# Turning the last keys right behind the result: two small TensorE jobs of one unit put into one run

## The chip, the cores and the metric

One core of a Trainium2 chip runs the whole program. The metric is the device time of one execution in microseconds (us), as the median of several executions. Beside it there is one profiled execution, in which the start and length of every instruction are recorded.

## The reference

Two stages follow each other. The first is a gated linear attention: for each of 4 batches and 8 heads a 48x48 state runs over 768 tokens. The second is a mixture of four two-layer networks on the first stage's result, 3072 rows of 384.

```python
for t in range(S):                                    # B, H, S, D = 4, 8, 768, 48
    state = alpha[:, :, t, :, None] * state + einsum('bhd,bhe->bhde', k[:, :, t], v[:, :, t])
    y[:, :, t] = einsum('bhd,bhde->bhe', q[:, :, t], state)
...
p = domain_probs / (domain_probs.sum(-1, keepdims=True) + 1e-09)
for e in range(4):                                    # x: (3072, 384), w1: 384x1024, w2: 1024x384
    h = np.maximum(x @ w1[e], 0.0)
    out += p[:, e:e + 1] * (h @ w2[e])
```

## The kernel before

**Two kinds of work on one TensorE.** The tokens are cut into 24 units (6 blocks of 128 tokens times 4 batches), numbered from 0 here, so the eleventh unit is unit 10. Units form groups of 2, 4, 4, 4, 4, 4 and 2. The network works through one group after another, for each of the four experts an up layer (`up`, products L775 of 512 columns into `one`) and a down layer (`down`, products L847 of 384 columns into `ops`). The attention of the later units is spread between these products. Where the network is at work, TensorE executes long stretches of L775 and L847, and every few microseconds a short run of attention products.

**The attention of one unit** is a generator with 17 steps, `attention(u)`. Each `yield` ends a step. The steps that matter here, by their number:

- steps 3 to 6 and 8 to 10 prepare levels of decayed queries and keys. ScalarE copies queries into `qb` (L541) and keys into `KT` (L559), VectorE multiplies (L548, L550, L560).
- step 7 makes the products of four levels (L567, 64 matrix passes in the trace, called P below), and step 11 those of the far half (L623, F) and of two levels more (L567).
- steps 12 and 13 copy `far` and `near` into `lat` on ScalarE (L636, L640).
- step 14, `turn_keys`: four turns of the last keys on TensorE (L287, T) into a PSUM tile, and a copy of it into `AT` on ScalarE (L683). It does nothing for the last block of a batch (units 20 to 23).
- step 15, `result`: the products of the unit's result (L662, R), which read `lat`, the queries and the state, and a copy of the result on ScalarE into `x_raw` (L675), or into `AT` in the last group (L679).
- step 16: the product of the turned keys and the values (L697, S), four VectorE operations that bring the state up to date (L707, L708), and the load of the values for two units later on SyncE's DMA queue.

T, R, S, F and P name these runs below. A number behind a letter is the count of matrix passes that the trace shows: T4, R56, S8 (or S16, where two halves are made apart), F8 and P64 or P32.

**When a step is issued** is worked out in advance. `deal()` gives every step of every unit a due time as a share of the unit's span: step 13 at 0.80, 14 at 0.87, 15 at 0.94 and 16 at 1.0 (`BEATS`), or 0.67, 0.755, 0.84 and 1.02 for units 11 to 17 (`IN_PAIRS`). `TOGETHER = ((15, 7), (16, 11))` sets, for these units, the due time of the next unit's step 7 to that of this unit's step 15, and of the next unit's step 11 to that of this unit's step 16. The steps are sorted by due time, and `advance` issues them as the estimated cost of the network's products passes. Nothing else reorders: every engine executes its instructions in the order in which they were issued.

**Buffers on the way.** The PSUM tiles of T, R and S share two buffers (tag `w`). `x_raw` has one buffer: the first copy of a group's result waits until `split_x` (L734 on ScalarE, L271 on VectorE) has read the group before. `attention` sets `in_runs = 10`, from which unit on the inputs are loaded as runs and transposed by VectorE (L488).

Of the kernel before, what the change touches and what calls it, by code (L numbers as in the profile page):

```python
# [20 lines left out]
def kernel(  # L21
# [94 lines left out]
    half = B // 2  # L116
# [47 lines left out]
    in_runs = 10  # L164
# [119 lines left out]
    def turned(src):  # L284
        tp = ps.tile([P, NP, P], F32, name="tp", tag="w")
        for p in range(NP):
            nc.tensor.transpose(tp[:, p, :], src(p), ident)  # L287
        return tp
# [187 lines left out]
    def attention(u):  # L476
# [171 lines left out]
        def result():  # L648
            yps = ps.tile([P, KC, P], F32, name="yps", tag="w")
            strips = [[] for _ in range(P // QUAD)]  # L650
            for c in range(KC):
                for j, strip in enumerate(strips):
                    p, part = divmod(len(strips) * c + j, 3)
                    terms = [(flat_st[:, p, QUAD * part:QUAD * (part + 1)], QT[:, p, :])] if cb > 0 else []
                    for i in range(2):
                        if part != 2 * (1 - i):
                            at = VD * (2 * p + i) + QUAD * part - D * i
                            terms.append((flat_v[:, at:at + QUAD], lat[:, 2 * p + i, :]))
                    strip += [(c, n == 0, n == len(terms) - 1, *term) for n, term in enumerate(terms)]
            for turn in zip(*strips):  # L660
                for j, (c, begins, ends, lhsT, rhs) in enumerate(turn):
                    nc.tensor.matmul(yps[QUAD * j:QUAD * (j + 1), c, :], lhsT=lhsT, rhs=rhs,  # L662
                                     start=begins, stop=ends)
            gi, slot = place[cb, b]
            if slot == 0:
                if gi == 0:
                    xTs[gi] = work.tile([P, 3, KC, NT], F32R, name="xT", bufs=1)
                    xraws[gi] = xTs[gi][:, 2].bitcast(F32)
                elif gi < LAST:
                    xraws[gi] = work.tile([P, KC * NT + PAD], F32, name="x_raw", bufs=1)[:, :KC * NT]  # L670
                    xraws[gi] = xraws[gi].rearrange("p (c n) -> p c n", n=NT)
                else:
                    xraws[gi] = []
            if gi < LAST:
                nc.scalar.copy(out=xraws[gi][:, :, slot * P:(slot + 1) * P], in_=yps)  # L675
            else:

                xraws[gi].append(AT)
                nc.scalar.copy(out=AT[:, :KC, :], in_=yps)  # L679

        def turn_keys():
            if cb < NCB - 1:
                nc.scalar.copy(out=AT, in_=turned(lambda p: KT[:, p, :]))  # L683


        for step in (turn_keys, result) if u >= half else (result, turn_keys):
            step()
            yield

        if cb < NCB - 1:  # L690
            KB = AT
# [203 lines left out]
    def deal():  # L895
# [15 lines left out]
        for gis in [*([gi] for gi in range(1, LAST - 1)), [LAST - 1, LAST]]:  # L911
# [6 lines left out]
            for k in range(n):  # L918
                u = sum(map(len, groups[:gi])) + k
                end = due - (n - 1 - k) * space  # L920
                begin = max(end - 2 * space, ends[-2])
                ends.append(end)
                run = attention(u)
                pairs = u in in_pairs
                beats = [0.0, *(IN_PAIRS if pairs else BEATS)]
                due_at = {-1: begin, **{j: begin + (end - begin) * beats[j + 1] for j in (7, 11, 16)}}
                for ahead, j in TOGETHER if pairs else ():
                    if (u > in_pairs[0] or j == 11) and abs(times[-1][ahead] - due_at[j]) < space / 6:
                        due_at[j] = times[-1][ahead]

                marks = sorted(due_at)
                times.append([])
                for lo, hi in zip(marks, marks[1:]):
                    times[-1] += [due_at[hi] if j == hi else
                                  due_at[lo] + (due_at[hi] - due_at[lo]) * (beats[j + 1] - beats[lo + 1])
                                  / (beats[hi + 1] - beats[lo + 1]) for j in range(lo + 1, hi + 1)]

                for j, ahead in ((6, 13), (12, 15)):
                    if times[:-1]:
                        times[-1][j] = max(times[-1][j], times[-2][ahead] + 0.5)  # L940
                events += [(time, u, run) for time in times[-1]]
# [8 lines left out]
    with tc.manual_schedule():  # L950
# [22 lines left out]
        def fill(times, n=P):  # L973
            for _ in range(times):
                nc.tensor.matmul(idle[:, :n], lhsT=zeros[:, :P], rhs=zeros[:, :n], start=True, stop=True)

        runs = [None, attention(1)]
        fill(7)
        runs[0] = first_unit(fill, runs[1])
# [65 lines left out]
```

## Time and profile before

| | |
|---|---|
| median of 3 executions | 1033.85 us (1030.1 to 1035.3) |
| profiled execution | 1027.61 us, of which the span is 1025.7 us |
| granted TensorE clock, mean | 0.998 |
| busy share: TensorE, VectorE, ScalarE | 97%, 68%, 43% |
| DMA | 254 GB/s mean |

The page's engine names are PE (TensorE matmul), PEld (its weight load), DVE (VectorE), ACT (ScalarE), POOL (GpSimd) and SP (SyncE). A timeline line gives start, time covered, engine, source line, operation, out<-in with shapes, and the count. A bracket at its end gives idle time of the engine ahead of it and what released it. The ends of matmuls are modelled; their starts are recorded. The profiled execution lies 6.2 us below the median of the three.

### The profile page before, as it was taken

The page shows a single profiled execution, that of the slowest core. Times are in us where ns is not written, and L with a number is a line of the kernel's source. Part 1 is how long each engine was busy: PE and PEld are TensorE (multiplying, and loading weights), DVE is VectorE, ACT ScalarE, POOL GpSimd, SP SyncE. Part 2 cuts the span into 40 slices and gives each one's busy share as a digit, 9 for nine tenths or more (in the row PEclk, how much of TensorE's full clock was granted, in tenths as well). Part 3 has the DMA queues.
Part 4 walks back from the last instruction along what each step waited for, and adds up shares of the span by engine and source line. Part 5 has one row for each costly group of instructions (what it writes and reads, how often), then busy time and mean ns, then how long its engine had stood idle before and what let it go on. Part 6 is the DMA issues. An engine that isn't in the chain of part 4 may idle for free.

```text
span 1025.7 us, 21120 instructions
## 1 busy us (share of the span) xinstructions
PE 998.4 (97%) x8564; PEld 886.7 (86%) x8564; DVE 702.4 (68%) x1430; ACT 438.7 (43%) x961; POOL 36.1 (4%) x79
## 2 busy tenths in 40 slices
PE   8889999999999999999999999999999999999998
PEld 7667777988888799898898898888988989898998
DVE  5698879687979868677767666885877743434343
ACT  5687666365354444335443415444454332211111
POOL 2010000000000100000000000000000000000000
PEclk9999999999999999999999999999999999999999
DMA  9499699398988999789889759786796454454531
GB/s 214 135 387 282 201 359 338 107 337 265 322 284 249 317 296 330 284 253 317 287 259 334 235 214 385 263 274 261 212 365 250 170 205 184 185 195 174 221 149 47
DMA packets 155632, 260.19 MB, mean 254 GB/s; under 512 B 95216, under 2 KB 132464, under 8 KB 133520
## 3 DMA queue, kind: packets, MB, share of 16 engines
q1 hardware_dynamic: 149072, 216.44, 63.7%
q0 software_dynamic: 6016, 42.08, 10.2%
q8 instruction: 68, 1.11, 0.4%
q10 hardware_dynamic: 448, 0.33, 0.1%
q14 instruction: 28, 0.23, 0.1%
HBM read 216.35 MB, written 42.47 MB: 252 GB/s over the span
## 4 chain that ended last, share of the span: by engine, by line
PE 81%; DVE 11%; ACT 4%; issue 2%; DMA 0%; POOL 0%; DVEq 0%; SPq 0%; ACTq 0%; POOLq 0%
PE ops L847 35%; PE one L775 31%; PE sc L567 5%; PE yps L662 3%; PE one L769 2%; PE tp L287 2%; DVE w L252 2%; ACT qb L541 2%; DVE hT L805 1%; DVE hT L800 1%; DVE near L577 1%; DVE QT L548 1%; PE sps L697 1%; DVE w L253 1%; PE far L623 1%
## 5 line engine op out<-in xcount | busy, mean ns | idle before, releaser
L847 PE MATMUL ops<-w,hT 128*128 128x384 f32 x2112 | 381.8, 339 | 9.4 <-ACT hT L777 6.7
L847 PEld LDWEIGHTS ops<-w,hT 128*128 128x128 f32 x2112 | 366.4, 189 | 15.6 <-ACT hT L777 8.9
L775 PE MATMUL one<-xT,w 128*128 128x512 f32 x1440 | 342.8, 394 | 0.8 <-DVE acc L875 0.8
L775 PEld LDWEIGHTS one<-xT,w 128*128 128x128 f32 x1440 | 266.8, 188 | 58.3 <-DVE acc L875 1.2
L777 ACT ACTIVATE hT<-one 128x512 fp32r<-128x512 f32 (+1 forms) x192 | 107.9, 562 | 343.4 <-PE one L775 318.7
L800 DVE SCALAR_TENSOR_TENSOR hT<-one,hT 128x512 fp32r<-128x512 f32 (+1 forms) x192 | 122.3, 645 | 105.2 <-ACT hT L777 104.8
L541 ACT COPY qb<-QT 64x256 f32<-64x256 f32 x322 | 131.1, 407 | 88.7 <-DVE QT L518 44.9
L548 DVE TENSOR_TENSOR QT<-QT,AT 128x256 f32<-128x256 f32 x158 | 66.7, 422 | 85.9 <-ACT qb L541 85.1
L805 DVE SCALAR_TENSOR_TENSOR hT<-hT 128x512 fp32r<-128x512 f32 (+1 forms) x192 | 112.8, 640 | 0.1
L577 DVE COPY_PREDICATED near<-masks,sc 128x256 f32<-128x256 uint8 x138 | 73.9, 536 | 41.5 <-PE sc L567 38.1
L567 PEld LDWEIGHTS sc<-qb,KT 128*64 128x64 f32 x2208 | 69.7, 138 | 7.3 <-issue 5.7
L567 PE MATMUL sc<-qb,KT 128*64 128x64 f32 x2208 | 74.0, 223 | 0.9 <-ACT qb L541 0.9
L875 DVE SCALAR_TENSOR_TENSOR acc<-ops,p_all,acc 128x384 f32<-128x384 f32 x66 | 40.0, 614 | 42.8 <-PE ops L847 42.8
L560 DVE TENSOR_TENSOR KT<-KT,AT 128x256 f32<-128x256 f32 x161 | 67.4, 418 | 0.0
L559 ACT COPY KT<-KT 128x256 f32<-128x256 f32 x138 | 57.5, 416 | 3.3
L769 PE MATMUL one<-xT,w 128*128 128x256 f32 (+1 forms) x240 | 46.2, 340 | 0.4 <-ACT xT L460 0.4
L847 PE MATMUL ops<-hT 128*128 128x384 f32 x128 | 46.2, 494 | 0.0
L550 DVE TENSOR_TENSOR AT<-AT 128x256 f32<-128x256 f32 (+1 forms) x138 | 39.1, 284 | 4.7
L769 PEld LDWEIGHTS one<-xT,w 128*128 128x128 f32 x240 | 37.7, 191 | 4.9 <-ACT xT L460 0.6
L884 POOL DMA_DIRECT2D out_dram<-acc x22 | 11.9, 540 | 673.7 <-DVE acc L875 673.7
L662 PE MATMUL yps<-lat,rv 128*32 128x128 f32 x736 | 33.1, 273 | 1.6 <-ACT lat L640 1.6
L775 PE MATMUL one<-KT,w 128*128 128x256 f32 x288 | 34.6, 279 | 0.0
(119 smaller groups left out, 709.1 us busy)
## 6 DMA issues: line engine op xcount, KB each, us to landing
w<-kept SPq DMA_DIRECT2D x140, 1152.0 KB, 8.8
kept<-w POOLq DMA_DIRECT2D x32, 1152.0 KB, 8.7
hT<-in_moe_w_dram SPq DMA_DIRECT2D x36, 384.0 KB, 5.9
w<-in_moe_w_dram SPq DMA_DIRECT2D x16, 384.0 KB, 5.8
rv<-in_v_dram SPq DMA_DIRECT2D x24, 192.0 KB, 9.3
out_dram<-acc POOLq DMA_DIRECT2D x22, 192.0 KB, 6.4
rk<-in_k_dram SPq DMA_DIRECT2D x14, 192.0 KB, 6.1
rq<-in_q_dram SPq DMA_DIRECT2D x14, 192.0 KB, 3.0
```

Source lines behind the costliest of these rows:

```text
L541: nc.scalar.copy(out=qb[rows, :, i, :].rearrange("p a (b r) -> p a b r", r=m), in_=qv[rows])
L548: nc.vector.tensor_mul(qv, qv, spread(dv[:, :, :, 0], m))
L560: nc.vector.tensor_mul(new[:, :, :, 0, :], old[:, :, :, 0, :], spread(halved(decs[li])[:, :, :, 1], m))
L567: nc.tensor.matmul(out[HALF * s:HALF * (s + 1), 2 * p:2 * p + 2, :], lhsT=KTs[li][:, p, HALF * s:HALF * (s + 1)], rhs=qbs[li][:, p, :, QUA ...
L577: nc.vector.copy_predicated(near.rearrange("p a (b two r) -> p a b two r", two=2, r=m)[:, :, :, 1, :], mk.unsqueeze(1).broadcast_to([P, H, ...
L662: nc.tensor.matmul(yps[QUAD * j:QUAD * (j + 1), c, :], lhsT=lhsT, rhs=rhs, start=begins, stop=ends)
L769: nc.tensor.matmul(one, lhsT=w[:, kc], rhs=xraws[gi][:, kc, lo:hi], start=(kc == 0), stop=(kc == KC - 1))
L775: nc.tensor.matmul(one, lhsT=w[:, part, kc], rhs=x_part(gi, part, kc), start=(part == 1 and kc == 0), stop=(part == 0 and kc == KC - 1))
L777: nc.scalar.activation(out=parts[0], in_=one, func=ACT.Relu, scale=TRIM)
L800: nc.vector.scalar_tensor_tensor(out=low, in0=x, scalar=0.0, in1=top.bitcast(F32), op0=ALU.max, op1=ALU.subtract)
L805: nc.vector.scalar_tensor_tensor(out=dif, in0=low.bitcast(F32), scalar=-4096.0, in1=top.bitcast(F32), op0=ALU.mult, op1=ALU.add)
L847: nc.tensor.matmul(sums[slot], lhsT=h, rhs=w, start=(n == begins[slot]), stop=(n == ends[slot]))
```

## The change

From unit 10 on, `result` runs first, `turn_keys` directly behind it, and one `yield` ends both. Earlier units keep two steps. Since one `yield` is gone, a later unit has 16 steps: R and T stand at step 14's due time, and what was step 16 (S, the state, the load of values) moves to step 15's. The due times themselves are not changed, so step 16's due time is left without work.

```diff
-        for step in (turn_keys, result) if u >= half else (result, turn_keys):
-            step()
+        if u >= in_runs:
+            result()
+            turn_keys()
             yield
+        else:
+            for step in (turn_keys, result) if u >= half else (result, turn_keys):
+                step()
+                yield
```

The order of issue on TensorE, without the network's products between the runs, one run per bracket:

```
            before                                    after
unit 10     [T] [R] [S F P32]                         [R T] [S] [F P32]
units 11-16 [T] [R P64] [S F P32]                     [R T] [S P64] [F P32]
unit 17     [T] [R] [S] [P64]                         [R T] [S] [P64]
unit 18     [T] [R P64] [S]                           [R T] [S P64]
unit 19     [T] [P64 R] [S]                           [R T] [P64 S]
units 20-22 [R P64]                                   [R] [P64]
unit 23     [R]                                       [R]
```

The P64 of a row belongs to the next unit, and so do the F and P32 of units 11 to 16. Over the whole program there are 110 such runs before and 110 after.

## The prediction

> **What bounds the kernel now.** The page's first part comes first, and with it the chain that ended last.
>
> ```profile
> PE 998.4 (97%) x8564; PEld 886.7 (86%) x8564; DVE 702.4 (68%) x1430; ACT 438.7 (43%) x961; POOL 36.1 (4%) x79
> ...
> PE ops L847 35%; PE one L775 31%; PE sc L567 5%; PE yps L662 3%; PE one L769 2%; PE tp L287 2%; DVE w L252 2%; ACT qb L541 2%; DVE hT L805 1%; DVE hT L800 1%; DVE near L577 1%; DVE QT L548 1%; PE sps L697 1%; DVE w L253 1%; PE far L623 1%
> ```
>
> TensorE is busy for 97% of the span, and its products are most of the chain. So the change is worth what it alters in TensorE's own stream, plus what it alters in the few stretches in which TensorE waits. I therefore read TensorE's timeline run by run, and then looked for its waits behind 290 us, where unit 10 begins to be affected.
>
> The runs stand alone at unit 17 (columns as in the table's legend):
>
> ```profile
> 607.24 0.60 PE L287 MATMUL tp<-ident,KT 128*128 128x128 f32 x4
> 607.60 5.97 PE L847 MATMUL ops<-w,hT 128*128 128x384 f32 x33
> 613.41 2.24 PE L775 MATMUL one<-xT,w 128*128 128x512 f32 x9
> ...
> 617.24 10.51 PE L775 MATMUL one<-xT,w 128*128 128x512 f32 x45
> 627.59 1.03 PE L697 MATMUL sps<-rv,AT 128*128 128x96 f32 x8
> 628.40 2.32 PE L775 MATMUL one<-xT,w 128*128 128x512 f32 x9
> 630.65 2.08 PE L567 MATMUL sc<-qb,KT 128*64 128x64 f32 x64
> 632.66 2.33 PE L775 MATMUL one<-xT,w 128*128 128x512 f32 x9
> ```
>
> Inside a stretch the network's products start every 226.7 ns (L775) or 173.3 ns (L847). From 613.41 to 617.24 are 3.83 us; nine products take 2.04, so R costs about 1.8 there. Behind R and P the second product comes 335 ns after the first, not 227, so a run's price must be read past its end. I took, for every run, the start of the last network product ahead of it and of the fourth behind it, less the pitches. The values repeat within 0.02 us: T4 0.447, R56 1.875, P64 2.228, R56P64 joined 3.908, F8P32 1.727 to 1.735, S16F8P32 joined 2.201, S8 0.908.
>
> Two things follow. Joining R and P saves 1.875 + 2.228 - 3.908 = 0.195 us: one opening and closing of a run. And T has hardly any such cost: four turns at 109 ns are 0.436 of its 0.447.
>
> **TensorE's stream, part by part.** T goes from a run of its own to the end of R's. It saves between 0 and 0.195 us, or loses as much if the turn from R to T is dearer than from R to the network. I take 0, since T alone opens and closes for 0.011. The Trainium skill (TensorEngine Tiling (Array Packing), Tiling Modes, Key Properties) says that changing the tiling mode drains the engine. By it T (128*128, like the network) still has a change to R (128*32) before it and saves nothing, whereas a fixed price per run would give 0.195 back; the trace agrees, with 0.011 for T and 0.195 for R or P.
>
> S16 (128*64 in the trace) leaves F and P32 (128*64) and joins P64 (128*64). It costs 2.201 - 1.731 = 0.470 in a joined run, the same in both. R no longer joins P64. So for each of units 11 to 16: before 0.447 + 3.908 + 2.201 = 6.556; after (1.875 + 0.447) + (2.228 + 0.470) + 1.731 = 6.751; +0.195.
>
> Unit 17: the same runs, only T moves: 0. Unit 18 and unit 19: R and P64 part (+0.195), and S8 (128*128) joins P64, which I value like T at 0 (bounds 0 to 0.195 saved): +0.195 each. Units 20 to 22 have no turned keys, so R alone moves ahead and parts from P64: +0.195 each. Together 6 + 2 + 3 = 11 partings: **+2.15 us**, from 0.0 (nine joins of R and T and two of S8 at full saving, -2.15) to 3.9 (the nine at full loss). Unit 10 has such a price too (S16 alone), but there TensorE waits anyway.
>
> **ScalarE at unit 10.** From 337 to 360 us TensorE is not the bound:
>
> ```profile
> 339.02 0.60 ACT L777 ACTIVATE hT<-one 128x512 fp32r<-128x512 f32 x1 [3.21 <-PE one L775]
> 339.51 0.58 ACT L683 COPY AT<-tp 128x512 f32<-128x512 f32 x1
> 339.98 0.82 ACT L541 COPY qb<-QT 64x256 f32<-64x256 f32 x2
> ...
> 340.83 0.42 DVE L548 TENSOR_TENSOR QT<-QT,AT 128x256 f32<-128x256 f32 x1 [2.46 <-ACT qb L541]
> ...
> 343.59 0.42 DVE L548 TENSOR_TENSOR QT<-QT,AT 128x256 f32<-128x256 f32 x1 [0.38 <-ACT qb L541]
> ...
> 357.93 0.60 ACT L777 ACTIVATE hT<-one 128x512 fp32r<-128x512 f32 x1 [7.05 <-DVE w L253]
> ...
> 358.58 0.44 PE L847 MATMUL ops<-w,hT 128*128 128x384 f32 x1 [1.73 <-ACT hT L777]
> 359.82 2.35 PE L847 MATMUL ops<-w,hT 128*128 128x384 f32 x12 [0.80 <-ACT hT L777]
> ```
>
> VectorE waits 2.46 us for `qb`, which stands behind the copy of the turned keys on ScalarE. From 343.59 it has no gap until 357.5 (splitting weights, L252 and L253), and TensorE then waits for it until 359.82, some 3 us in two gaps. After the change R stands ahead of T at 338.6, and ScalarE's copy of R stands ahead of that of T and of `qb`. R ends 1.76 us later than T would have begun, so `qb` moves from 339.98 to about 341.7, and every step of the chain by 1.7. The copy of R itself (0.48) fits into the time of the four turns. The gap of 0.38 returns behind the later TensorE products, so it absorbs nothing. Before, R ran at 343.1, beside VectorE's own work, and cost this chain nothing. So TensorE goes on at 361.5 instead of 359.82: **+1.7 us**, from 0 (something else holds the weights) to 2.2 (the copy does not fit). The four state operations (1.45 us) move ahead inside the same unbroken VectorE work: 0. Should that chain become shorter than TensorE's, unit 10's own +0.2 would show.
>
> **What lies hidden.** The other stretch with waits, 648 to 680, is set off by network products at 635.0 and 675.0, and the runs ahead of these keep their sum: 0. The copy of R now ahead of `qb` in units 11 to 22 makes the next P64 wait only if it takes the 4 to 8 us of network products between; at unit 14 this is tightest. There the copy has to wait for `x_raw`, which VectorE reads until 494.6 (L271), so ScalarE is held from 490.3; `qb` follows at 496.5, and P64 comes at 498.7: 0, and each us beyond a margin of 2.2 costs one. The load of values goes ahead of three to five weight loads on SyncE's queue. It waits for S alone, which precedes what frees those buffers, and takes about 1 us of the DMA engines; TensorE has no wait for DMA behind 290 us: 0. R needs `lat`. In unit 21 this is finished at 759.64 and R's first product with it moves from 763.49 to 759.68; units 22, 23 and 20 have 0.3, 0.3 and 0.9 us left, units 14 and 16 have 2: 0.
>
> **The sum.** 2.15 + 1.7 = 3.85 us. The profiled execution of 1027.61 would become 1031.5; the median of the runs shown lies 6.2 above that execution, and with the same distance it becomes 1033.85 + 3.85 = 1037.7.
>
> **Rivals.** *R meets an unfinished `lat`.* Place: units 20 to 23, then 14 and 16. It decides as soon as ScalarE is later against TensorE than the margins of 0.05, 0.3, 0.3 and 0.9 us. One us later costs 0.95 + 0.7 + 0.7 + 0.1 = 2.5 us: 1040.2, slower by 0.6%. For it: the margins are short and the ordinary executions are longer than the profiled one. Against it: the copies of `lat` are set off by the same TensorE products, so both move together.
>
> *Every join saves.* T behind R and S8 beside P64 give back 0.195 each, the sum on TensorE is 0 and only unit 10 costs: 1035.6; if unit 10's chain is also held by something else, 1033.9, no change at all. Against it: T's 0.011.
>
> *The early load helps.* Values loaded ahead let the inputs behind them land about 1 us sooner, and a late VectorE transpose is on the chain near 680: 1 us gained there, and with all joins saving and no loss at unit 10, 1032.9. Against it: only one of those waits reaches TensorE.
>
> **Chances and range.** Forecast 0.5 (its own range 1035.5 to 1040); unfinished `lat` 0.22; joins save 0.22; early load 0.06. A measurement can tell about 0.5%, 5.2 us, from no change: 1028.7 to 1039.0. Four fifths of the forecast's chance (0.40), a quarter of the first rival's (0.05), nearly all of the second's (0.21) and half of the third's (0.03) lie within: 0.69. Slower: 0.10 + 0.17 = 0.27; faster: 0.04. The range from 1032.5 to 1041.5 takes in the second rival, the first, and the ends of the unknown joins but for their extremes.
>
> **What would show it.** In the trace after: [R T] at 2.32 us and [S16 P64] at 2.70; P64 alone behind R alone in units 20 to 22; VectorE's wait for `qb` near 341 grown from 2.46 to about 4.1, and TensorE's gaps near 357 to 361 from 3 to 4.7; no wait of L662 for L640. It is wrong if [R T] costs 2.13 or less, if TensorE's gap at unit 10 stays, or if L662 shows waits.

## The result and the profile after

| | before | after |
|---|---|---|
| median of 20 executions each | 1031.92 us (1028.93 to 1035.3) | 1037.15 us (1034.05 to 1039.27) |
| ratio of after to before | | 1.0047, 95% interval 1.0037 to 1.0058 |
| profiled execution, and its span | 1027.61 us, 1025.7 us | 1037.45 us, 1035.6 us |
| granted TensorE clock, mean of the runs (before: of the 77 runs beside the experiments) | 0.9936 | 0.9918 |

The change makes the kernel slower by 0.0047 x 1031.92 = 4.85 us (3.8 to 6.0). Forecast were 1037.7 us and a sum of 3.85. That the predicted time lies within 0.6 us is luck in part: the three executions of before that were shown have a median 1.9 us above that of the twenty, and the sum is 1.0 too small; the two errors offset each other.

The page's first part of after, with the shares of its chain (lines behind the change stand five lines further down: L847 became L852, L775 L780, L777 L782, L697 L702):

```profile
PE 1006.4 (97%) x8564; PEld 890.8 (86%) x8564; DVE 703.4 (68%) x1430; ACT 438.5 (42%) x961; POOL 36.1 (3%) x79
...
PE ops L852 35%; PE one L780 29%; PE sc L567 5%; PE yps L662 3%; PE one L774 2%; PE tp L287 2%; DVE w L252 2%; ACT qb L541 2%; DVE hT L810 1%; DVE hT L805 1%; DMA w<-kept 1%; DVE QT L548 1%; DVE w L253 1%; DVE near L577 1%; PE sps L702 1%
```

TensorE has as many instructions as before and is busy for 8 us more: the same products took longer. One entry of this list is new, a DMA of weights (`w<-kept`, 1%).

The two traces differ by 9.9 us, twice what the medians do. Laid side by side by the starts of their products, after's network products are already 4.05 us behind at 337 us, ahead of everything that the change moves. So only 5.85 us of the difference between the traces can belong to the change, and the size is taken from the medians.

Unit 17 in the timeline of after, TensorE alone:

```profile
618.19 0.66 PE L287 MATMUL tp<-ident,KT 128*128 128x128 f32 x4
618.61 5.97 PE L852 MATMUL ops<-w,hT 128*128 128x384 f32 x33
624.42 2.24 PE L780 MATMUL one<-xT,w 128*128 128x512 f32 x9
626.49 1.03 PE L702 MATMUL sps<-rv,AT 128*128 128x96 f32 x8
627.30 12.52 PE L780 MATMUL one<-xT,w 128*128 128x512 f32 x54
639.75 2.09 PE L567 MATMUL sc<-qb,KT 128*64 128x64 f32 x64
641.76 2.33 PE L780 MATMUL one<-xT,w 128*128 128x512 f32 x9
```

T4 now closes R's run; R's first product is at 616.53, the network's next at 618.61. From the last network product ahead to the fourth behind, less the pitches, as the prediction did it, the joined [R T] costs 2.264 to 2.275 us, against 1.875 + 0.447 = 2.322 apart.

Unit 10 in the timeline of after, lines of ScalarE, VectorE and TensorE as they answer to those of before:

```profile
343.06 0.60 ACT L782 ACTIVATE hT<-one 128x512 fp32r<-128x512 f32 x1 [3.20 <-PE one L780]
344.62 0.66 PE L287 MATMUL tp<-ident,KT 128*128 128x128 f32 x4
344.76 0.48 ACT L675 COPY x_raw<-yps 128x384 f32<-128x384 f32 x1 [1.10 <-PE yps L662]
345.32 0.59 ACT L683 COPY AT<-tp 128x512 f32<-128x512 f32 x1
345.80 0.82 ACT L541 COPY qb<-QT 64x256 f32<-64x256 f32 x2
346.65 0.42 DVE L548 TENSOR_TENSOR QT<-QT,AT 128x256 f32<-128x256 f32 x1 [4.14 <-ACT qb L541]
349.46 0.42 DVE L548 TENSOR_TENSOR QT<-QT,AT 128x256 f32<-128x256 f32 x1 [0.43 <-ACT qb L541]
...
363.60 0.60 ACT L782 ACTIVATE hT<-one 128x512 fp32r<-128x512 f32 x1 [7.93 <-DVE w L253]
364.25 0.44 PE L852 MATMUL ops<-w,hT 128*128 128x384 f32 x1 [3.08 <-ACT hT L782]
365.78 11.86 PE L852 MATMUL ops<-w,hT 128*128 128x384 f32 x52 [1.09 <-ACT hT L782]
```

The new copy into `x_raw` stands ahead of `AT` and `qb`; VectorE's wait grew from 2.46 to 4.14 us, and TensorE's two idle times behind it from 1.73 and 0.80 to 3.08 and 1.09. The last line holds what the prediction had not foreseen: 52 products in 11.86 us. Windows of after from there (length, then the busy time and count of PE, PEld, DVE, ACT and POOL, then the granted clock, the DMA share and GB/s):

```profile
360.00:366.00 6.00, 1.83 (x9) 1.25 (x8) 5.18 (x9) 2.06 (x5) 1.06 (x2) 0.88 0.99 410
366.00:372.00 6.00, 6.00 (x21) 6.00 (x22) 5.93 (x10) 2.62 (x6) 0.00 (x0) 0.55 1.03 361
372.00:378.00 6.00, 6.00 (x49) 5.75 (x51) 5.17 (x12) 1.47 (x4) 0.00 (x0) 1.00 1.08 251
```

From 366 to 372 TensorE is busy all the time, yet makes 21 products at a granted clock of 0.55, and in the next six microseconds 49 instructions at 1.00. Before, the eight microseconds behind the same waits were at full clock:

```profile
360.00:368.00 8.00, 8.00 (x47) 8.00 (x48) 7.90 (x14) 3.78 (x10) 0.00 (x0) 1.00 1.07 360
```

The half clock of after lasts from 364.6 to 371.4 us. In it L852's products start every 320 ns, not 173, and the distance to before grows from 5.96 to 8.54: 2.6 us in this trace.

So there are three theories for the 4.85 us. *Partings*: runs that shared one opening and closing now stand apart, 1.4 to 1.6 us. *Unit 10*: its longer wait, about 1.9. *Clock*: behind that wait TensorE loses clock. The first two are the prediction's, the third is new; the rival to it is that the half clock is a chance of this one trace.

### The profile page after: what moved, and what is told of

The parts are those of the page before. It is cut to its first block, busy times and chain, and to the rows that moved or that the text cites. A ratio compares the mean times of both kernels' runs of the same rounds, so it can differ in the third digit from the quotient of the medians.

```text
span 1035.6 us, 21115 instructions
## 1 busy us (share of the span) xinstructions
PE 1006.4 (97%) x8564; PEld 890.8 (86%) x8564; DVE 703.4 (68%) x1430; ACT 438.5 (42%) x961; POOL 36.1 (3%) x79
## 3 DMA queue, kind: packets, MB, share of 16 engines
q8 instruction: 68, 1.11, 0.4%
## 4 chain that ended last, share of the span: by engine, by line
PE 80%; DVE 12%; ACT 4%; issue 2%; DMA 1%; SPq 0%; POOL 0%; DVEq 0%; ACTq 0%; POOLq 0%
PE ops L852 35%; PE one L780 29%; PE sc L567 5%; PE yps L662 3%; PE one L774 2%; PE tp L287 2%; DVE w L252 2%; ACT qb L541 2%; DVE hT L810 1%; DVE hT L805 1%; DMA w<-kept 1%; DVE QT L548 1%; DVE w L253 1%; DVE near L577 1%; PE sps L702 1%
## 5 line engine op out<-in xcount | busy, mean ns | idle before, releaser
L852 PE MATMUL ops<-w,hT 128*128 128x384 f32 x2112 | 385.4, 341 | 12.7 <-ACT hT L782 8.3
L852 PEld LDWEIGHTS ops<-w,hT 128*128 128x128 f32 x2112 | 368.9, 190 | 19.7 <-ACT hT L782 10.5
L780 PE MATMUL one<-xT,w 128*128 128x512 f32 x1440 | 342.2, 393 | 0.3 <-DVE hT L805 0.3
L780 PEld LDWEIGHTS one<-xT,w 128*128 128x128 f32 x1440 | 266.9, 188 | 57.5 <-DVE hT L805 1.0
L782 ACT ACTIVATE hT<-one 128x512 fp32r<-128x512 f32 (+1 forms) x192 | 107.9, 562 | 344.0 <-PE one L780 322.4
L541 ACT COPY qb<-QT 64x256 f32<-64x256 f32 x322 | 131.1, 407 | 92.0 <-DVE QT L518 44.9
L559 ACT COPY KT<-KT 128x256 f32<-128x256 f32 x138 | 57.4, 416 | 3.3
L852 PE MATMUL ops<-hT 128*128 128x384 f32 x128 | 46.2, 494 | 0.0
L780 PE MATMUL one<-KT,w 128*128 128x256 f32 x288 | 34.6, 279 | 0.0
```

Of the source, the lines that this page charges most:

```text
L541: nc.scalar.copy(out=qb[rows, :, i, :].rearrange("p a (b r) -> p a b r", r=m), in_=qv[rows])
L780: nc.tensor.matmul(one, lhsT=w[:, part, kc], rhs=x_part(gi, part, kc), start=(part == 1 and kc == 0), stop=(part == 0 and kc == KC - 1))
L782: nc.scalar.activation(out=parts[0], in_=one, func=ACT.Relu, scale=TRIM)
L852: nc.tensor.matmul(sums[slot], lhsT=h, rhs=w, start=(n == begins[slot]), stop=(n == ends[slot]))
```

## The experiments

**The two parts alone.** The first kernel leaves unit 10 as before, the second changes unit 10 only.

```diff
-        if u >= in_runs:
+        if u > in_runs:          # first kernel
+        if u == in_runs:         # second kernel
```

> The change from unit 11 on; unit 10 keeps its two steps. Theory: the loss has two parts, the partings of units 11 to 22 on TensorE (about 1.6 us by the trace after) and the longer wait of TensorE at unit 10 with what the granted clock loses behind it (2 to 4.5 us). Here only the first is left: 1.6 us slower than before, ratio about 1.0016, and TensorE's two gaps at the first down layer of the third group as before (about 3.0 us over the pitch). Rival: the loss lies in units 11 to 22 (waits of later stretches), unit 10's gap being covered elsewhere: ratio 1.004 or more.

> The change at unit 10 alone. Theory: TensorE's two gaps grow from 3.0 to about 4.9 us, and the rest of the trace keeps its runs: 2 us slower, up to 4.5 where the granted clock drops behind the gap; ratio 1.002 to 1.004. Rival (all of it in the later units): ratio 1.000.

Measured: from unit 11 on 1.0010 (0.9995 to 1.0026); unit 10 alone 1.0023 (1.0007 to 1.0039). The first lines are the timeline of the kernel from unit 11 on, the second ones that of unit 10 alone:

```profile
343.46 0.42 DVE L548 TENSOR_TENSOR QT<-QT,AT 128x256 f32<-128x256 f32 x1 [2.70 <-ACT qb L541]
361.21 0.44 PE L852 MATMUL ops<-w,hT 128*128 128x384 f32 x1 [1.74 <-ACT hT L782]
362.45 9.29 PE L852 MATMUL ops<-w,hT 128*128 128x384 f32 x52 [0.79 <-ACT hT L782]
```

```profile
344.87 0.43 DVE L548 TENSOR_TENSOR QT<-QT,AT 128x256 f32<-128x256 f32 x1 [4.22 <-ACT qb L541]
362.48 0.44 PE L852 MATMUL ops<-w,hT 128*128 128x384 f32 x1 [3.08 <-ACT hT L782]
```

The longer wait comes with unit 10's order alone. From unit 11 on the waits are those of before, no half clock follows them, and the network products of this trace fall back 1.4 us over units 11 to 22 (from 2.6 to 4.0 behind those of before). With unit 10 alone the half clock stands at 363.3 us for 6.8 us, as in after; one window:

```profile
364.00:370.00 6.00, 5.99 (x19) 5.99 (x20) 5.93 (x9) 2.63 (x7) 0.00 (x0) 0.50 1.03 383
```

**Is it ScalarE's copy?** The prediction named the copy of R ahead of `qb` among its reasons for unit 10's loss. In this kernel unit 10 turns the keys first, R's products follow in the same run, and their copy comes one step later, behind `qb`. Units 11 on are as before.

```diff
+            if u == in_runs:               # in result(), in place of the copy
+                return lambda: nc.scalar.copy(out=xraws[gi][:, :, slot * P:(slot + 1) * P], in_=yps)
...
-        if u >= in_runs:
-            result()
-            turn_keys()
+        if u == in_runs:
+            turn_keys()
+            copy = result()
             yield
+            copy()
```

> At unit 10 alone: keys turned first and the result directly behind in one run, and ScalarE's copy of the result issued one step later, so that the copies of the queries stand behind the copy of the turned keys alone. If it is ScalarE's copy of the result in the queue that delays VectorE (the prediction's wording), VectorE's wait near 340 us is 2.5 us as before, its second one 0.4, TensorE's gaps stay at 3.0 us and the ratio is 1.000. If it is the 1.8 us of result products ahead of the network's products, whose results ScalarE waits for before the next copies of queries, the first wait is 2.5, the second grows from 0.4 to about 2, the gaps are 4.7 us and the ratio 1.002 to 1.004, as with the change at unit 10 alone.

Measured: 1.0030 (1.0014 to 1.0045). Its timeline:

```profile
345.71 0.43 DVE L548 TENSOR_TENSOR QT<-QT,AT 128x256 f32<-128x256 f32 x1 [2.38 <-ACT qb L541]
350.34 0.42 DVE L548 TENSOR_TENSOR QT<-QT,AT 128x256 f32<-128x256 f32 x1 [2.24 <-ACT qb L541]
365.44 0.44 PE L855 MATMUL ops<-w,hT 128*128 128x384 f32 x1 [3.38 <-ACT hT L785]
```

The first wait is back at 2.4 us, but the second grew from 0.38 to 2.24, and TensorE's gap is as long as in after. R's 1.8 us on TensorE now stand ahead of the network products whose result ScalarE must take up before its next `qb`. So the delay is R's time ahead of this chain, by whichever of two paths; the places of T and of the copy only choose the path. This kernel moves both, and none leaves R ahead of T and moves the copy alone. But the trace of after speaks against the copy there too: it ends at 345.24, and T behind R ends at 345.28 (344.62 + 0.66, a modelled end), so `AT` at 345.32 waits for T.

**Does filling the wait keep the clock?** If the half clock follows from TensorE's idle time, products of no use in that time should prevent it. They multiply the identity and write to a tile that nobody reads. The first kernel had products of 384 columns, the second of 128.

```diff
+            if (gi, e) == (2, 0) and n in (6, 7):
+                spin = ps.tile([P, DM], F32, name="spin", tag="w")
+                for _ in range(9 if n == 6 else 4):
+                    nc.tensor.matmul(spin, lhsT=ident, rhs=ident_all[:, :1].broadcast_to([P, DM]), start=True, stop=True)
```

```diff
+            for _ in range({(2, 0, 6): 14, (2, 0, 7): 5}.get((gi, e, n), 0)):
+                spin = ps.tile([P, P], F32, name="spin", tag="w")
+                nc.tensor.matmul(spin, lhsT=ident, rhs=ident, start=True, stop=True)
```

> The whole change, and 13 products of no use (384 columns, about 0.33 us each) in TensorE's two gaps at unit 10: 9 ahead of the seventh product of that down layer, 4 ahead of the eighth. Theory: the idle time of almost 5 us is what lowers the granted clock behind it (half for 6.8 us in the trace after, about 2.6 us lost); filled, the clock stays full there and the run is 1 to 3 us faster than with the change as it is, ratio 1.002 to 1.004. Rival: the drop of the clock has nothing to do with this gap: the time is that of the change, ratio 1.005, or a little more.

> The whole change, with TensorE's two gaps at unit 10 filled by short products of no use (128 columns, about 0.22 us each): 14 in the first gap (3.1 of 3.25 us), 5 in the second (1.1 of 1.36). In the filled run before, the fill was 3.5 us too long, and the half clock behind the gap was gone. Theory (idle time lowers the clock): no half-clock stretch near 365 us in the trace, and 1 to 2.6 us faster than the change as it is: ratio 1.002 to 1.004. Rival (the gap alone counts): ratio 1.005.

Measured: 1.0077 (1.0059 to 1.0096) and 1.0031 (1.0019 to 1.0043). The fill of the first, then of the second:

```profile
359.42 6.00 PE L855 MATMUL spin<-ident 128*128 128x384 f32 x18
365.43 2.75 PE L855 MATMUL spin<-ident 128*128 128x384 f32 x8
```

```profile
360.51 3.88 PE L854 MATMUL spin<-ident 128*128 128x128 f32 x28
364.41 1.48 PE L854 MATMUL spin<-ident 128*128 128x128 f32 x10
```

Thirteen products of 384 columns became 26 passes, and a product cost about 0.6 us (nine in the 5.54 us from 359.42 to 364.96), twice what they had been sized for. They outlast the waits by about 3.5 us, so the first kernel's time tells only that. The second kernel's fill fits, and its windows run at full clock throughout:

```profile
360.00:366.00 6.00, 6.00 (x45) 5.80 (x45) 5.21 (x9) 2.53 (x6) 0.99 (x2) 1.00 1.00 419
366.00:372.00 6.00, 6.00 (x37) 6.00 (x36) 5.93 (x9) 2.31 (x5) 0.00 (x0) 1.00 1.04 367
```

Neither trace has a half clock near 365. The order of work is after's, the wait of the chain is after's, and the filled kernel stands at 1.0031, not 1.0047: 1.6 us less, though the two intervals overlap, so the size is not sure.

**Other orders of the same runs.** R, T and P64 in one run at the time where R and P64 met before, with T in the middle or in front:

```diff
         if u >= in_runs:
+            yield
             result()             # first kernel; the second has the two calls swapped
             turn_keys()
             yield
```

> The result and the turned keys behind it from unit 10 on, but both at the due time of step 15, so that the next unit's products stay behind them in one run (R, T, P) and the state's product stays with the far half. If the drain by array mode holds, T between R and P takes away what the joining of R and P saved: R56T4P64 costs about 4.4 to 4.5 us against 0.447 + 3.908 = 4.355 before, 0.1 us more for each of seven units. Unit 10: the copy of the turned keys no longer stands ahead of the queries, so VectorE's wait near 340 us and TensorE's gaps shrink by up to 0.5 us. Ratio 1.000. Rival (a run has one fixed price): the seven units gain 0.15 us each, ratio 0.998.

> As the one with R, T, P, but the keys are turned ahead of the result: T, R, P in one run. By array mode T ahead of R costs what it costs behind network products, R and P stay joined: 4.30 to 4.36 us for the run, no loss in the seven units; unit 10 as there, up to 0.5 us gained. Ratio 0.999 to 1.000, the best of all orders if anything is gained. Rival: T with R in front delays the copies behind it, as the change did at unit 10: ratio 1.002.

Measured: [R T P] 1.0016 (1.0002 to 1.0030), [T R P] 0.9998 (0.9984 to 1.0011). By the same reading of prices the run costs 4.48 to 4.50 us in the first and 4.33 to 4.35 in the second (units 11 to 16 and 18); before, T4 and R56P64 cost 0.447 + 3.908 = 4.355. First [R T P], then [T R P]:

```profile
380.26 0.66 PE L287 MATMUL tp<-ident,KT 128*128 128x128 f32 x4
380.85 2.08 PE L567 MATMUL sc<-qb,KT 128*64 128x64 f32 x64
```

```profile
380.97 0.60 PE L287 MATMUL tp<-ident,KT 128*128 128x128 f32 x4
...
383.16 2.09 PE L567 MATMUL sc<-qb,KT 128*64 128x64 f32 x64
```

In the first, T (128\*128) stands between R (128\*32) and P (128\*64): P starts 0.59 us behind T's start, where four turns take 0.44. In the second, P follows R directly. So T between the two small tilings costs as much as parting them does (2.27 for [R T] and 2.225 for P64 alone are 4.495), and T in front costs nothing. Unit 19 is the cross-check, because P stands first there: the first kernel makes [P R T], at 4.29 us, the second [P T R], at 4.49. Both kernels have R behind the chain of unit 10 again (VectorE's first wait 1.90 and 1.97 us).

**Filling the waits of before.** If lost clock is lost time, a fill should make the kernel before faster too. It was filled at the waits near 312 and 359 us; the second kernel below does much the same, and at 284 us as well, to the order [T R P].

```diff
+            for _ in range({(1, 3, 6): 6, (1, 3, 7): 6, (2, 0, 6): 8, (2, 0, 7): 4}.get((gi, e, n), 0)):
+                spin = ps.tile([P, P], F32, name="spin", tag="w")
+                nc.tensor.matmul(spin, lhsT=ident, rhs=ident, start=True, stop=True)
```

> The kernel before, with short products of no use in two of its waits: the down layer of the second group's last expert (6 and 6, in gaps of 1.45 and 1.36 us) and that of the third group's first (8 and 4, in gaps of 1.9 and 1.07 us). Theory (idle time lowers the granted clock): the half-clock stretch of 3.4 us near 313 to 316 us, seen in most traces, is gone, worth 1.7 us: ratio 0.998 to 0.999, faster than both kernels. Rival: no change, ratio 1.000, or a loss of some tenths of a us.

> The best order so far (T, R, P in one run from unit 10 on) with short products of no use in three waits of TensorE: the second group's third expert (2 and 6 products in gaps of 0.6 and 1.6 us late in its down layer), its fourth (6 and 6) and the third group's first (6 and 4, in gaps of 1.45 and 1.07 us). If idle time lowers the clock, the half-clock stretches near 287 and 317 us go, 1.7 us each: ratio 0.997 to 0.998, faster than both kernels. Rival: they go and others come, or the fill costs as much: ratio 1.000.

Measured: before filled 0.9997 (0.9984 to 1.0009) at a mean clock of 0.9964; [T R P] filled 0.9988 (0.9973 to 1.0003) at 0.9982. The clock rose as expected, the time hardly fell, and no version is shown to beat before. One reason can be read: before's trace has half clock at 313.4 for 3.4 us, and no wait of TensorE near 330. With the fill TensorE arrives early there and waits for VectorE:

```profile
331.83 0.44 PE L850 MATMUL ops<-w,hT 128*128 128x384 f32 x1 [0.35 <-DVE hT L805]
332.43 1.83 PE L850 MATMUL ops<-w,hT 128*128 128x384 f32 x9 [0.16 <-DVE hT L805]
```

Counted by starts, these two waits take 0.51 and 0.43 us: 0.9 of the 1.3 us that a stretch of 3.4 us at half clock costs (half of the 2.6 above) is given back at once. Another loss is in both filled traces and in no other: TensorE waits at 766.15 and 764.56 us (1.11 and 0.67 us idle), put down to ScalarE's copies for the next unit (L559, L541). What sets these waits off stays open.

**The load of values.** After shows a wait for weights from DMA, 1.35 us, which the prediction had not:

```profile
646.50 9.43 PE L852 MATMUL ops<-w,hT 128*128 128x384 f32 x53 [1.35 <-DMA w<-kept]
```

This kernel is after with the load of values at its old place among SyncE's DMAs.

```diff
+        if u >= in_runs:
+            yield
         load(u + 2, "v")
         yield
```

> The whole change, but from unit 10 on the load of values is issued at the due time of step 16 again, in the place on SyncE's queue that it has before the change. In the trace after the change TensorE waits 1.4 us for a weight load near 645 us, which it does not before. If it is the load of values ahead of the weights that makes this piece late, the wait is gone, TensorE's waits for VectorE near 658 and 664 us (less by 1.5 us after the change) come back, and the time between the network products at 640 and 664 us stays. If it is the shifted time of the other loads, the wait of 0.5 to 2 us stays.

Measured once: 1034.13 us. The wait stays:

```profile
642.81 9.44 PE L854 MATMUL ops<-w,hT 128*128 128x384 f32 x53 [1.01 <-DMA w<-kept]
```

So the early load of values is not its cause. A wait there, of 0.5 to 2.0 us, is also in the traces of the kernels from unit 11 on, with the copy later, with both fills of after and with [R T P], and not in those of unit 10 alone, [T R P] with or without fill, and before filled; what sets it off stays open. It costs nothing at the end: before, TensorE waits for VectorE at 649.42 and 654.87 (0.39 and 0.85 us idle); in after these waits are gone, and the distance between the traces goes from 9.10 to 10.70 and back to 9.13.

**Clock and time over all runs.** Every run has its mean clock. Over 196 runs, 77 of before and 119 of the ten kernels that were run several times, one straight line for each kernel with a common slope fits with 0.97 us left over: 7.4 us (6.7 to 8.2) for each 0.01 of clock. What a kernel costs at the clock of before is then

| kernel | mean clock | against before, as run | at equal clock |
|---|---|---|---|
| after | 0.9918 | +4.87 | +3.56 ± 0.50 |
| from unit 11 | 0.9941 | +1.23 | +1.58 ± 0.60 |
| unit 10 only | 0.9927 | +2.49 | +1.85 ± 0.60 |
| copy later | 0.9923 | +2.79 | +1.84 ± 0.60 |
| after, filled to size | 0.9951 | +2.68 | +3.80 ± 0.69 |
| [R T P] | 0.9938 | +1.30 | +1.46 ± 0.60 |
| [T R P] | 0.9945 | -0.29 | +0.37 ± 0.60 |
| before, filled | 0.9964 | -0.27 | +1.82 ± 0.63 |
| [T R P], filled | 0.9982 | -1.21 | +2.24 ± 0.68 |

(us; differences of means; ± is a 95% bound; the fill that was too long is left out. The slope is a correlation between runs, not a setting of the clock.) At equal clock the two parts add up to after: 1.58 + 1.85 = 3.43 against 3.56. The rest, 0.0018 of clock or 1.3 us, is what the change loses in clock. The filled version of after has the same price at equal clock as after, so what it gains goes with the clock. The last rows warn of the slope: filling before raised the clock by 0.0028, worth 2.1 us by it, and 0.3 came out. It prices lost clock fairly only where the time is not given back at the next wait. Behind unit 10 it is not given back: in the traces of after and of unit 10 alone the distance to before is not made good later.

## Why the prediction was right, and where not

**Partings, 2.15 us forecast.** Right in kind, a third too large: 1.6 by prices, 1.4 by the products' offset (from 8.54 us at 368 to 9.90 at 832), 1.58 ± 0.60 at equal clock. [S P64] came at 2.69 to 2.70 (forecast 2.70), P64 alone at 2.22 to 2.23, R alone at 1.87. The mis-sized term is T's join, valued at nothing: it saves 2.322 - 2.268, about 0.055, in each of nine units, and S8 ahead of P64 saves 0.05 (3.088 against 3.136), though in unit 19, behind P64, only 0.015 (3.121). A unit from 11 to 16 thus costs 6.694 against 6.556, 0.14 and not 0.195. [R T] at 2.27 stays well above the 2.13 that would have made the step wrong. The rival *every join saves* falls: 0.055 of its 0.195.

The rows give the pattern: a join of two small tilings (R with P) saves 0.195, a join with a 128\*128 run 0.015 to 0.055, and T set between R and P costs 0.15 more than T in front. The Trainium skill (TensorEngine Tiling (Array Packing), Key Properties) says that a change of tiling mode drains the engine. The orders agree: [T R P] has one change fewer among its runs than [R T P]. So does S16, of P64's own tiling: alone, at unit 10, it costs 0.815, so joined with P64 it saves 0.815 + 2.228 - 2.695 = 0.35, with two changes fewer. The 0.05 is not in that rule.

**Unit 10, 1.7 us forecast.** The size was right: VectorE's wait 4.14 (forecast 4.1), TensorE's gaps counted by starts 4.6 us (forecast 4.7), TensorE's next stretch 1.9 us later against the products ahead, unit 10 alone 1.85 ± 0.60 at equal clock. The step named two reasons: "ScalarE's copy of R stands ahead of that of T and of `qb`" is so, but with it away from there the loss stayed. It is the other, "R ends 1.76 us later than T would have begun": R's time on TensorE, from which the step had taken its size.

**The term that was missing.** The sum ended with TensorE going on at full clock. Behind the grown wait it went on at half clock, 2.6 us lost in this trace, 1.3 us over the runs. The evidence is this: stretches of half clock at 363 to 366 us stand in the traces of after, of unit 10 alone and of the kernel with the copy later (6.8 us each), and of the one with the values' load as before (3.4 us), all with 3.1 to 3.4 us of idle time in one piece; none in the two filled ones, in before or from unit 11 on. With the idle time filled and all else the same the half clock is gone from the trace, in two kernels. But no length of wait decides it alone: [R T P], with 1.59 and 0.79, has 3.4 us of half clock there too, and the waits at 284 and 315 us are followed by one in some traces and not in others.

The traces also record when the granted clock changed, and one rule fits all twelve. In each trace the starts of half clock lie whole multiples of 3.413 us apart, to within 0.01 us. Cut on that grid into windows, from 270 us on, where the network keeps TensorE busy, the twelve traces have 20 windows at full clock with half clock behind them, and TensorE is idle for at least 1.64 us in every one. Of the 2562 with full clock behind them, one has 1.65 us idle and none of the others more than 1.56. (Ahead of 270 us the line is less clean: half clock behind 1.05 us idle at 13 us in after, none behind 1.99 at 63 us in the kernel with the values' load as before.) The nearest cases and the largest:

| trace | window (us) | idle in it | clock in the next window |
|---|---|---|---|
| before | 357.82 to 361.23 | 1.56 | 1.00 |
| from unit 11 | 282.31 to 285.73 | 1.65 | 1.00 |
| [R T P] | 359.67 to 363.08 | 1.64 | 0.50 |
| before | 310.03 to 313.44 | 2.01 | 0.50 |
| after | 361.19 to 364.60 | 3.07 | 0.50 |

A window at half clock has a second one behind it in three cases, with 0.67 us idle in it or more, and none in twenty, with 0.58 or less. So what counts in these traces is how much idle time falls into one window, and the dividing line lies near half of it. Where the borders fall differs from trace to trace, and that is the chance in it. Before's trace was lucky at unit 10: its 2.5 us of idle time were divided between two windows. With the grid slid over the trace in small steps, half clock beginning at 1.7 us idle and going on at 0.6 (an estimate), before has 0.9 windows of half clock there on average and after 1.7, always at least one. The 0.8 more, at 1.3 us each, are 1.0 of the 1.3 us; filled it is none, which forecasts 0.0015 more mean clock than before (measured 0.9951 against 0.9936).

The Trainium skill (TensorE: Matmul & The Clock Gate, Part 1) has a gate that goes to half after an idle window of some 3.4 us, counted by windows that run freely. The lengths here, 3.4 and 6.8 us, agree, and so does the grid. The bound does not: before's trace has half clock at 313.4 behind two waits of 1.28 and 1.10 us with a product between.

**What was called hidden.** At unit 14 ScalarE is held for `x_raw`, and no wait of TensorE follows:

```profile
503.52 0.48 ACT L675 COPY x_raw<-yps 128x384 f32<-128x384 f32 x1 [5.53 <-DVE xT L271]
```

The stretch from 648 to 680 cost nothing, though one wait took the place of others. The load of values put back leaves a run of 1034.13 us at a clock of 0.995; at after's 0.9918 that is 1034.13 + 0.0032 x 744 = 1036.5 (estimated by the slope), within a microsecond of after's 1037.15. So it shows neither a cost nor the rival's gain. The rival *unfinished `lat`* did not occur (waits view: total, times, longest; first after, then before):

```profile
PE yps L662 <- ACT lat L640: 1.4, 3, 0.8
```

```profile
PE yps L662 <- ACT lat L640: 1.6, 3, 0.8
```

These are the same early waits in both; in units 14 to 23 there is none.

**The sum.** 1.6 + 1.9 + 1.3 = 4.8 us against 4.85 measured; forecast 2.15 + 1.7 + 0 = 3.85. One term was too large, one a little small, one absent. The 1.3 is what the fit leaves of after's loss, so the close sum is no test of it; the filled run's 1.6 us less and the count of windows are.

## What to carry to other kernels

When two small jobs trade places ahead of one that others wait for, price the time of the one that now goes first on the busy engine, not only the copy that it leaves on the next. Look at TensorE's tilings before joining runs: a job in the network's own tiling belongs at the edge of a run, not between two small tilings. And where a change lengthens a wait of TensorE, look at the granted clock behind it, and at how much idle time a window of 3.4 us can hold; compare kernels at equal clock over many runs, since here 0.01 of clock was 7 us.

## What the runs showed of the hardware

- Behind waits of 3.1 and 1.1 us with a single product between them the granted clock was half for 6.8 us, with products every 320 ns in place of 173. Products of 128 columns in the wait kept it at 1.00.
- Half clock starts on a grid of 3.413 us within a trace, from 270 us on behind windows of that length in which TensorE was idle for at least 1.64 us (20 of 20); behind 2561 windows with at most 1.56 us idle it never started, and once not behind one with 1.65.
- The mean clock explains most of the spread from run to run: a correlation of -0.81 over the 77 runs of before and -0.89 over the 20 of after.
- Half clock ahead of a wait is partly free: 0.9 of 1.3 us came back as waiting when it was removed.
- The filling products of 384 columns, plain f32, took two passes and about 0.6 us each, those of 128 columns 0.26 us (14 in 3.64). The network's products of 384 columns, whose operand ScalarE writes as fp32r, start every 0.173 us.
